# Sparse attention and two MLPs in float32 on one core: the last eight blocks of the first MLP's output as products of quarters

## The chip, the cores and the metric

One core of one Trainium2 chip runs the kernel, in one launch. The metric is the device time of the program in microseconds (us). The kernel before takes 849.72 us, the median of three runs (847.67 to 850.36).

## The reference: what is computed

```python
scores = (1 / sqrt(64)) * q @ k.T            # 4 batches, 8 heads, 576 positions, head size 64
# heads 0-3 see the last 32 positions, heads 4-7 the earlier ones of the same residue mod 32
x = softmax(masked scores) @ v               # -> 2304 tokens x 512
h = x @ moe_w_in                             # first MLP, 512 -> 2048
x = (s * relu(h)**2 + b) @ moe_w_out         # 2048 -> 512, s and b are scalars
h = x @ moe2_w_in                            # second MLP, 512 -> 2048
g = where(h >= 1, h, where(h <= -1, 0, (h + 1)**2 / 4))
out = g @ moe2_w_out                         # 2048 -> 512
```

Everything is float32.

## The kernel before

**Products.** Each float32 operand is split into a high and a low part (hi, lo), and a product is three matmuls on TensorE: hi x hi, hi x lo, lo x hi (`mm3`, L680 to L684; `mm3s`, L929 to L934). The operand that moves is 128 x 384, the weight 128 x 128. ScalarE writes the high part (L310), VectorE or GpSimd subtracts it for the low part (L721, L351, L974).

**Tokens and blocks.** The 2304 tokens are six units of 384 (`UNITS`, NU = 6). The 2048 hidden features are 16 blocks of 128. The first MLP runs in two halves of eight blocks (MS = 8), and each half goes over all units. For one unit and block `hidden` makes the 128 features from the 512 inputs with 12 matmuls (L700), then relu (L704), square (L708 or L710), s and b (L715 or L717), and the split gh, gl (L310, L721). `output` multiplies them into four accumulators of 128 x 384 with 12 matmuls (L751). At the end of the first half the accumulators go to HBM as `part`; in the second half they are read back (`pi`, L745) and added, and the sums are written into x2 (L759), the input of the second MLP.

**Attention** is done in groups, in step with the first units of the first half (`attend_upto`).

**The second MLP** works on pairs of units (three pairs of 2 x 384 tokens) and halves of the features. Each product of 2 x 2 quarters is made as seven products of quarters and of sums of quarters (`PRODS`, Strassen's scheme in Winograd's form): "A11", "A12", "A22", "S1" to "S4" are weights, "B11" to "T4" inputs. `hidden2` and `output2` run them; the running results are combined in one PSUM bank per pair of positions. The sums of the weights are made once: `prepare` (L357 to L396) loads two blocks of raw weights, decodes them (L324 to L332), splits them (L376), forms the sums (L391) and writes all seven quarters, high and low, to HBM (`dw`, L379). Each later use loads one quarter, high and low together, with one 256 KB DMA (L855, rings w0h, w0l, w0hx, w0lx of four, sixteen in all). There are 16 preparations: six in the last unit of the first half (`EARLY`), ten in the second half.

**Raw weights** come as 512 KB loads of integers in two byte planes (`raw`, L324, ring of three), with two decode steps on VectorE (L330, L332) and one on ScalarE (L328).

**What sets the order.** `Issue` collects every operation with its engines, modelled costs, the buffers it needs, and a due time that is worked out backwards from its successors; `order()` takes the operation that can start first (then the one that is due first), and `emit` writes each engine's program in that order. So each engine has a fixed sequence. All of SP's DMAs are issued in order, and an issue that waits for its data or its buffer holds the ones behind it.

The seven products, in the order in which they run:

```python
PRODS = ((1, "A11", "B11"), (5, "S1", "T1"), (6, "S2", "T2"), (3, "S4", "B22"), (7, "S3", "T3"), (2, "A12", "B21"),
         (4, "A22", "T4"))
SUMS = {"T1": ("B11", "B12", "B11"), "T2": ("B11", "B22", "B11"), "T3": ("B12", "B22", "B12"), "T4": ("B21", "B21", "B11")}
```

## Time and profile before

| | |
|---|---|
| median of three runs | 849.72 us (847.67 to 850.36) |
| the profiled execution's own time | 847.82 us |
| its span | 846.0 us, mean granted TensorE clock 0.983 |
| TensorE busy | 824.3 us, 97%, 6336 instructions |
| VectorE busy | 599.4 us, 71%, 1250 instructions |
| ScalarE busy | 517.4 us, 61%, 1054 instructions |
| GpSimd busy | 22.8 us, 3%, 62 instructions |
| DMA | 191.77 MB, mean 227 GB/s |
| second half of the first MLP begins | 287.5 us |
| second MLP begins | 492.2 us |

The profile's busy time counts the durations of instructions; overlapping ones are counted once. PE is TensorE's matmul stream, PEld its weight loads, DVE VectorE, ACT ScalarE, POOL GpSimd, and SP the engine that issues most DMAs. The granted clock is given as a share of 2.4 GHz. The DMA share is the mean busy share of the core's 16 DMA engines.

### The profile page before, as it was taken

To read this page: it belongs to the slowest core of one execution; us is meant where nothing else is said; L and a number is where in the kernel's file an instruction comes from. 1 tells how busy PE (TensorE), PEld (TensorE's weight loads), DVE (VectorE), ACT (ScalarE), POOL (GpSimd) and SP (SyncE) were. 2 spreads that over 40 slices of the span, in tenths; PEclk is the share of its full clock that TensorE was granted. 3 is DMA by queue.
4 is the path that set the end of the run, shared out by engine and by line. 5 is a ranking of instruction groups with operands and counts; after the bars stand their busy time and mean duration, and the time that the engine had idled before them with its cause. 6 is when DMAs were issued, how large, how long until landed. Compare 5 with 4: busy or idle time off the path is not lost.

```text
span 846.0 us, 17391 instructions
## 1 busy us (share of the span) xinstructions
PE 824.3 (97%) x6336; PEld 800.7 (95%) x6336; DVE 599.4 (71%) x1250; ACT 517.4 (61%) x1054; POOL 22.8 (3%) x62
## 2 busy tenths in 40 slices
PE   6789999999999999999999999999999999999998
PEld 3579998989999899999999999999999999999998
DVE  5788647475598785767678356897666998465966
ACT  3577645554577674556567467875477854577653
POOL 1110000010000000000001000000000000000000
PEclk9599999999999999999999999999999999999999
DMA  8858271363389994768785558888988788878883
GB/s 260 259 177 276 99 240 64 91 183 108 122 289 329 277 310 132 223 222 255 257 303 196 154 185 253 252 255 271 293 267 256 252 254 286 289 252 252 251 271 103
DMA packets 115930, 191.77 MB, mean 227 GB/s; under 512 B 13830, under 2 KB 57990, under 8 KB 115846
## 3 DMA queue, kind: packets, MB, share of 16 engines
q1 hardware_dynamic: 114818, 190.23, 70.7%
q8 instruction: 51, 0.84, 0.4%
q10 hardware_dynamic: 1028, 0.43, 0.2%
q14 instruction: 33, 0.27, 0.1%
HBM read 150.25 MB, written 40.37 MB: 225 GB/s over the span
## 4 chain that ended last, share of the span: by engine, by line
PE 84%; DMA 8%; DVE 4%; ACT 2%; issue 1%; SPq 1%; ACTq 0%; DVEq 0%
PE h L682 7%; PE acc L682 6%; PE acc L684 6%; PE acc L683 6%; PE h L683 6%; PE h L684 6%; PE acc L934 6%; PE acc L932 6%; PE acc L933 6%; PE side L934 5%; PE side L933 5%; PE side L932 5%; DMA raw<-in_w_ins 4%; PE h L934 3%; PE h L932 3%; PE h L933 3%
## 5 line engine op out<-in xcount | busy, mean ns | idle before, releaser
L704 ACT ACTIVATE t<-h 128x384 f32<-128x384 f32 x96 | 46.5, 485 | 62.6 <-PE h L684 62.2
L682 PE MATMUL acc<-gh,w1hx 128*128 128x384 f32 x192 | 65.2, 340 | 0.0
L682 PE MATMUL h<-xh,w0hx 128*128 128x384 f32 x192 | 65.1, 339 | 0.0
L683 PE MATMUL acc<-gl,w1hx 128*128 128x384 f32 x192 | 64.9, 338 | 0.2
L683 PE MATMUL h<-xl,w0hx 128*128 128x384 f32 x192 | 64.5, 336 | 0.0
L684 PE MATMUL acc<-gh,w1lx 128*128 128x384 f32 x192 | 64.5, 336 | 0.0
L684 PE MATMUL h<-xh,w0lx 128*128 128x384 f32 x192 | 64.2, 334 | 0.0
L310 ACT ACTIVATE gh<-t 128x384 fp32r<-128x384 f32 x96 | 50.0, 521 | 21.9 <-DVE t L717 21.3
L721 DVE TENSOR_TENSOR gl<-t,gh 128x384 fp32r<-128x384 f32 x92 | 51.0, 555 | 16.1 <-ACT gh L310 15.8
L717 DVE TENSOR_SCALAR t<-t,fix_t 128x384 f32<-128x384 f32 x77 | 36.7, 477 | 35.8 <-ACT t L708 35.5
L682 PE MATMUL acc<-gh,w1h 128*128 128x384 f32 x168 | 57.2, 340 | 0.0
L684 PE MATMUL acc<-gh,w1l 128*128 128x384 f32 x168 | 56.9, 339 | 0.0
L683 PE MATMUL acc<-gl,w1h 128*128 128x384 f32 x168 | 56.8, 338 | 0.0
L682 PE MATMUL h<-xh,w0h 128*128 128x384 f32 x144 | 50.8, 353 | 0.2 <-ACT t L704 0.2
L683 PE MATMUL h<-xl,w0h 128*128 128x384 f32 x144 | 49.4, 343 | 0.0
L684 PE MATMUL h<-xh,w0l 128*128 128x384 f32 x144 | 49.3, 342 | 0.0
L708 ACT ACTIVATE t<-t 128x384 f32<-128x384 f32 x79 | 41.4, 524 | 2.1
L683 PEld LDWEIGHTS acc<-gl,w1hx 128*128 128x128 f32 x192 | 36.0, 188 | 1.1 <-DVE gl L721 1.0
L682 PEld LDWEIGHTS acc<-gh,w1hx 128*128 128x128 f32 x192 | 36.0, 188 | 0.4
L682 PEld LDWEIGHTS h<-xh,w0hx 128*128 128x128 f32 x192 | 36.0, 188 | 0.3
L683 PEld LDWEIGHTS h<-xl,w0hx 128*128 128x128 f32 x192 | 36.1, 188 | 0.0
L684 PEld LDWEIGHTS h<-xh,w0lx 128*128 128x128 f32 x192 | 36.1, 188 | 0.0
(513 smaller groups left out, 2514.3 us busy)
## 6 DMA issues: line engine op xcount, KB each, us to landing
w0h<-dw SPq DMA_DIRECT2D x84, 256.0 KB
w0l<-dw SPq DMA_DIRECT2D x84, 256.0 KB
w0hx<-dw SPq DMA_DIRECT2D x84, 256.0 KB
w0lx<-dw SPq DMA_DIRECT2D x84, 256.0 KB
raw<-in_w_ins SPq DMA_DIRECT2D x32, 512.0 KB
raw<-in_w_outs SPq DMA_DIRECT2D x32, 512.0 KB
dw<-pt SPq DMA_DIRECT2D x48, 256.0 KB
dw<-po SPq DMA_DIRECT2D x48, 256.0 KB
```

What stands on the lines that cost most here:

```text
L310: e.activation(out=out, in_=in_, func=AF.Copy)
L682: e.matmul(out=acc, lhsT=wh, rhs=ah, start=first, stop=False)
L683: e.matmul(out=acc, lhsT=wh, rhs=al, start=False, stop=False)
L684: e.matmul(out=acc, lhsT=wl, rhs=ah, start=False, stop=last)
L704: op(lambda e: e.activation(out=c(t), in_=c(p), func=AF.Relu), [act(n)], [p], [t])
L708: e.activation(out=c(t), in_=c(t), func=AF.Square)
L717: e.tensor_scalar(out=c(t), in0=c(t), scalar1=sb_t[:, 0:1], scalar2=sb_t[:, 1:2], op0=MUL, op1=ADD)
L721: op(lambda e: e.tensor_tensor(out=c(gl), in0=c(t), in1=c(gh).bitcast(F32), op=SUB), [pool(n)] + [dve2(n)], [t, gh], [gl])
L932: e.matmul(out=dst, lhsT=wh, rhs=ah, start=opens and first, stop=False, skip_group_check=not opens)
L933: e.matmul(out=dst, lhsT=wh, rhs=al, start=False, stop=False, skip_group_check=not opens)
L934: e.matmul(out=dst, lhsT=wl, rhs=ah, start=False, stop=last, skip_group_check=not opens)
```

## The change

The last eight blocks of the first MLP are computed in pairs of units. `first_steps(p)` makes the hidden features of a pair directly, as before, but keeps each block's 128 x 384 result whole in SBUF (`inner`: the homes of w_out's weights for pairs 0 and 2; the homes xl of the first units, pi, t and dt for pair 1). `second_steps(p)` then makes the output as the seven products, each over KQ = 4 pairs of blocks with six matmuls (`product`, which `output2` now uses too). Gates are summed for T1 to T4 and every factor is split for each product in which it stands. The partial sums of a unit come into x2 by one DMA (L1021), and the products' running results are added to them (L1034, 14 additions for a pair). Its prepared weights are a third set, dw[2], four preparations more (20 for 16), loaded into a ring of six (`S_TAGS`).

The order of the stages is: first half; hidden of pair 0; outputs of pair 0 between the hidden products of pair 1; outputs of pair 1 between the hidden products of pair 2; outputs of pair 2 alone; second MLP. Seven preparations stand in units 1 to 3 of the first half (`AT_FIRST`), twelve in the last eight blocks (`AT_HALF`), one at the start of the second MLP (`AT_NEXT`). The input weights of the last eight blocks are decoded during the last unit of the first half.

Besides, the planner now knows eight DMAs outstanding (`LANES`), the first batch's side loads of the attention are issued by GpSimd instead of ScalarE and merged into fewer DMAs, fix_t is the first load of ScalarE's queue, po's ring has four buffers instead of two, and the T matrices of the second MLP all stand in the homes xl and xh.

```diff
-EARLY = 6
+KQ = MS // 2
+AT_FIRST = {(1, 6): 1, (2, 0): 1, (2, 3): 1, (2, 6): 1, (3, 1): 1, (3, 4): 1, (3, 7): 1}
+AT_HALF = {(0, 0): 1, (0, 2): 1, (0, 4): 1, (0, 6): 1, (1, 1): 1, (1, 3): 1, (1, 5): 1, (1, 7): 1, (2, 1): 1, (2, 3): 1, (2, 5): 1, (2, 7): 1}
+AT_NEXT = {0: 1}
...
+S_TAGS = ["kb"] * 4 + ["qx", "sx"]
+SPLIT, SUMMED, SUM_BACK, EVAC2 = (0.0, 6.0, 6.0), (0.0, 0.0, 0.0), 0, 5.0
...
+LANES = 8
...
+                    if o.dmas and e != "pool":
+                        at = max(at, lanes[o.dmas - 1] - DMA_ISSUE * (o.dmas - 1))
...
-        op(lambda e: e.dma_start(out=fix_t, in_=fixed[:, 128 + KT:FW]), [("act", 0.5, DMA_LATENCY)], writes=[fix_buf]).sooner = 50.0
-        op(lambda e: [e.dma_start(out=mask_t[g * 64:g * 64 + 54, 0:54], in_=fixed[0:54, 0:54]) for g in range(2)],
-           [("act", 1.0, DMA_LATENCY)], part=[mask_buf[0]]).sooner = 49.0
+        op(lambda e: e.dma_start(out=fix_t, in_=fixed[:, 128 + KT:FW]), [("act", 0.5, DMA_LATENCY)], writes=[fix_buf], dmas=1).sooner = 80.0
+        op(lambda e: e.dma_start(out=mask_t[:, 0:54], in_=bass.AP(fixed.tensor, fixed.offset, [[0, 2], [FW, 64], [1, 54]])),
+           [("act", 0.5, DMA_LATENCY)], part=[mask_buf[0]], dmas=1).sooner = 49.0
...
-        side = ("act", b_line) if b == 0 else ()
+        side = ("pool", b_line) if b == 0 else ()
...
-    def hidden(g, u):
+    def hidden(g, u, whole=None):
         n = UNITS[u]
         p = buf(ps, "h", [128, UMAX], F32, 2)
-        t = buf(sp, "t", [128, UMAX], F32, TB)
-        gh = buf(sp, "gh", [128, UMAX], F32R, LAG + 1)
-        gl = buf(sp, "gl", [128, UMAX], F32R, LAG + 1)
+        if whole:
+            t, own = whole, [whole]
+        else:
+            t = buf(sp, "t", [128, UMAX], F32, TB)
+            gh = buf(sp, "gh", [128, UMAX], F32R, LAG + 1)
+            gl = buf(sp, "gl", [128, UMAX], F32R, LAG + 1)
+            own = [t, gh, gl]
...
+        if o == 2:
+            tag = S_TAGS[loads[1] % len(S_TAGS)]
+            y = buf(sp, tag, [128, 2, 256], F32R, BUFS[tag])
+        else:
+            tag = ("w0h", "w0l", "w0hx", "w0lx")[loads[0] % 4]
+            y = buf(wp, tag, [128, 2, 256], F32R, MS // 2)
+        loads[o == 2] += 1
...
+    blocks = []
+
+    def sum_after(o):
+        return blocks[-SUM_BACK:][:1] if o == 2 and SUM_BACK else ()
+
+    def product(o, k, a, b, g_of, dst):
+        for i in range(counts[o]):
+            home = b
+            if b in SUMS:
+                home, l, r = SUMS[b]
+                d, l, r = (g_of[i, v] for v in (home, l, r))
+                op(lambda e, d=d, l=l, r=r: e.tensor_tensor(out=d.tile, in0=l.tile, in1=r.tile, op=SUB),
+                   [dve2(n), pool(n)], [v for v in (l, r) if v is not d], [d], after=sum_after(o)).sooner = SUMMED[o]
+            g = g_of[i, home]
+            hi = buf(sp, "gh", [128, n], F32R, LAG + 1)
+            lo = buf(sp, "gl", [128, n], F32R, LAG + 1)
+            op(lambda e, g=g, hi=hi: copy(e, hi.tile, g.tile), [act(n)], [g], [hi], allocs=[lo], line=g_line)
+            op(lambda e, g=g, hi=hi, lo=lo: e.tensor_tensor(out=lo.tile, in0=g.tile, in1=hi.tile.bitcast(F32), op=SUB),
+                   [pool(n), dve2(n)], [g, hi], [lo]).sooner = SPLIT[o]
+            w = wmat(o, i, a)
+
+            def f(e, dst=dst, w=w, hi=hi, lo=lo, k=k, i=i):
+                for c in range(2):
+                    wc = [w.tile[:, v, c * 128:(c + 1) * 128] for v in range(2)]
+                    mm3s(e, dst[c].tile, wc, (hi.tile, lo.tile), k in START, i == 0, i == counts[o] - 1)
+
+            pe_block(f, [w, hi, lo], dst)
+            blocks.append(chain[0])
+            yield
+
+    halves, spares, mixed = [{} for _ in range(PAIRS)], {}, []
+
+    def spare(tag):
+        if tag not in spares:
+            spares[tag] = const.tile([128, KD, NP], F32, name=f"g_{tag}", tag=tag)
+        return spares[tag]
+
+    def inner(p, m, u):
+        if p != 1:
+            return buf(wp, ("w1h", "w1l")[u % 2] + ("" if m < KQ else "x"), [128, n], F32, MS // 2)
+        j = 2 * m + u % 2
+        if j < 2 * KD:
+            return Part(lambda: spare(f"xl{j // KD}")[:, j % KD, :])
+        tag = (["pi"] * KD + ["t"] * TB + ["dt"])[j - 2 * KD]
+        return buf(sp, tag, [128, n], F32, {"pi": KD, "t": TB, "dt": DT}[tag])
+
+    def first_steps(p):
+        us = (2 * p, 2 * p + 1)
+        for g in range(MS, 2 * MS):
+            m = g - MS
+            make(0, g + 1)
+            for u in us:
+                y = halves[p][m % KQ, f"B{m // KQ + 1}{u % 2 + 1}"] = inner(p, m, u)
+                hidden(g, u, y)
+                if pend:
+                    output(*pend.pop(0))
+                yield
+            for _ in range(AT_HALF.get((p, m), 0)):
+                prepare(*todo.pop(0))
+
+    def second_steps(p):
+        us = (2 * p, 2 * p + 1)
+        slot = {u: [Buf(None, None) for _ in range(KD)] for u in us}
+        for u in us:
+            op(lambda e, u=u: e.dma_start(out=x2[u].tile, in_=part_d[u].rearrange("c p n -> p c n")), [dma(KD * n * 512)],
+               part_buf[u], slot[u], after=[x_last[u]], allocs=[x2[u]])
+        sets = [[buf(ps, t, [128, NP], F32, 2 if t == "side" else 1) for t in ts]
+                for ts in (("side", "side"), ("acc0", "acc1"), ("acc2", "acc3"))]
+        x, z, y = sets[p % 3:] + sets[:p % 3]
+        for k, a, b in PRODS:
+            dst = {1: x, 6: x, 7: x, 4: x, 5: z, 3: z, 2: y}[k]
+            yield from product(2, k, a, b, halves[p], dst)
+            r, t, ends = {1: (1, 0, 0), 5: (2, 1, 0), 6: (1, 1, 0), 3: (1, 1, 1), 7: (2, 1, 1), 2: (1, 0, 1), 4: (2, 0, 1)}[k]
+            u = us[t]
+            for c in range(2):
+                j = c + 2 * (r - 1)
+                d = slot[u][j]
+                op(lambda e, u=u, j=j, s=dst[c]: e.tensor_tensor(out=x2[u].tile[:, j, :], in0=s.tile, in1=x2[u].tile[:, j, :],
+                                                                 op=ADD),
+                   [dve(n)], [dst[c]], [d], part=touched(u, j) if ends else ()).sooner = EVAC2
...
+            if u == NU - 1:
+                make(0, MS + g + 1)
+            for _ in range(AT_FIRST.get((u, g), 0)):
+                prepare(*todo.pop(0), early=u < NU - 1)
...
+    list(first_steps(0))
+    for p in range(PAIRS):
+        more, done_, step = first_steps(p + 1) if p + 1 < PAIRS else iter(()), 0, 0
+        for _ in second_steps(p):
+            step += 1
+            while done_ < step * 2 * MS / (7 * KQ):
+                next(more, None)
+                done_ += 1
+        list(more)
+        if p == 1:
+            mixed.append(chain[0])
```

SP's queue in the last eight blocks. Before, writes of prepared weights (dw), raw loads and the partial sums of one unit:

```order
L745 DMA pi_5380<-part_79 128x384
L745 DMA pi_5393<-part_79 128x384
L745 DMA pi_5399<-part_79 128x384
L745 DMA pi_5410<-part_79 128x384
L324 DMA raw_5420<-in_w_outs 128x512
L379 DMA dw_2_92<-pt_5412 128x2x256
L379 DMA dw_2_92<-po_5413 128x2x256
L379 DMA dw_3_93<-po_5429 128x256
L379 DMA dw_3_93<-pt_5428 128x256
L379 DMA dw_2_92<-pt_5479 128x2x256
L379 DMA dw_3_93<-pt_5486 128x2x256
L379 DMA dw_2_92<-po_5480 128x2x256
```

After, the same queue while pair 1's outputs are made: the loads of kb, qx and sx are the prepared weights of the products (dw_0 to dw_3 of the third set), between the writes of others:

```order
L851 DMA kb_5968<-dw_2_100 128x512
L851 DMA kb_5978<-dw_3_101 128x512
L394 DMA dw_3_93<-po_5906 128x2x256
L394 DMA dw_3_93<-po_5893 128x2x256
L394 DMA dw_4_94<-pt_5992 128x256
L394 DMA dw_4_94<-po_5993 128x256
L851 DMA qx_6025<-dw_0_98 128x512
L394 DMA dw_4_94<-pt_6010 128x2x256
L851 DMA sx_6043<-dw_1_99 128x512
L394 DMA dw_4_94<-po_6011 128x2x256
L851 DMA kb_6073<-dw_2_100 128x512
L851 DMA kb_6089<-dw_3_101 128x512
```

Loads that TensorE waits for soon now stand behind writes that wait for ScalarE's pt and VectorE's po.

VectorE in the last eight blocks. Before, affines (L717), splits gl (L721) and the steps of the preparations (L330, L332, L376):

```order
L717 TENSOR_SCALAR t_5490<-t_5490,fix_t 128x384
L376 TENSOR_TENSOR po_5544<-sm_5341,pt_5543 128x512
L721 TENSOR_TENSOR gl_5492<-t_5490,gh_5491 128x384
L330 TENSOR_SCALAR qv_5518<-qv_5518 128x512
L710 TENSOR_TENSOR t_5537<-t_5537 128x384
L332 SCALAR_TENSOR_TENSOR qv_5518<-raw_5517,qv_5518 128x512
L376 TENSOR_TENSOR po_5571<-sm_5340,pt_5570 128x512
L721 TENSOR_TENSOR gl_5539<-t_5537,gh_5538 128x384
L330 TENSOR_SCALAR qv_5519<-qv_5519 128x512
L376 TENSOR_TENSOR po_5606<-qv_5518,pt_5605 128x256
L332 SCALAR_TENSOR_TENSOR qv_5519<-raw_5560,qv_5519 128x512
L717 TENSOR_SCALAR t_5586<-t_5586,fix_t 128x384
```

After, at the same place of the program (L735 affine, L974 split of a product's factor, L351 and L353 decode, L391 and L406 preparation, L1034 addition of a result to x2):

```order
L406 TENSOR_TENSOR qv_5497<-qv_5497,qv_5496 128x256
L351 TENSOR_SCALAR sm_5695<-sm_5695 128x512
L353 SCALAR_TENSOR_TENSOR sm_5695<-raw_5694,sm_5695 128x512
L735 TENSOR_SCALAR w1l_5715<-w1l_5715,fix_t 128x384
L974 TENSOR_TENSOR gl_5759<-pi_5111,gh_5758 128x384
L351 TENSOR_SCALAR sm_5696<-sm_5696 128x512
L974 TENSOR_TENSOR gl_5774<-pi_5212,gh_5773 128x384
L353 SCALAR_TENSOR_TENSOR sm_5696<-raw_5697,sm_5696 128x512
L391 TENSOR_TENSOR po_5781<-qv_5497,pt_5780 128x512
L391 TENSOR_TENSOR po_5789<-qv_5496,pt_5788 128x512
L1034 TENSOR_TENSOR x_3_5449<-acc_948_5454,x_3_5449 128x384
L1034 TENSOR_TENSOR x_3_5449<-acc_949_5455,x_3_5449 128x384
```

The splits are now one for each product block, and the additions stand between them.

SP's queue at the start, with the semaphores that an issue waits for in brackets. Before:

```order
L447 DMA xh_2_131<-in_strd 128x764 x2
L447 DMA w0hx_148<-in_strd 54x2x256 x2
L447 DMA xl_15_157<-in_strd 128x2x764 [waits DMAHW0_49]
L447 DMA w0lx_193<-in_strd 54x2x256 [waits DMAHW5_49]
L447 DMA w0lx_193<-in_strd 54x2x256 [waits DMAHW7_49]
L447 DMA xh_37_203<-in_loc 128x896 [waits DMAHW1_49]
L447 DMA xl_38_236<-in_loc 128x896 [waits DMAHW4_49]
```

After:

```order
L461 DMA xh_2_134<-in_strd 128x764 x2
L461 DMA w0hx_153<-in_strd 54x2x256 x2
L461 DMA xl_15_166<-in_strd 128x2x764
L461 DMA w0lx_196<-in_strd 54x2x256
L461 DMA w0lx_196<-in_strd 54x2x256 [waits DMAHW0_49]
L461 DMA xh_37_203<-in_loc 128x896 [waits DMAHW1_49]
L461 DMA xl_38_236<-in_loc 128x896 [waits DMAHW2_49]
```

The load of xl and the first half of the load of w0lx lose their waits; the other waits are for other lanes.

## Rows read from the trace of the kernel before

**Rows 1.** Page: busy time by engine; the chain that ended last, by engine.
```profile
PE 824.3 (97%) x6336; PEld 800.7 (95%) x6336; DVE 599.4 (71%) x1250; ACT 517.4 (61%) x1054; POOL 22.8 (3%) x62
...
PE 84%; DMA 8%; DVE 4%; ACT 2%; issue 1%; SPq 1%; ACTq 0%; DVEq 0%
```

**Rows 2.** Busy by stretch: us, PE, PEld, DVE, ACT, POOL, PEclk, DMA share, GB/s.
```profile
42.00:120.00 78.00, 74.58 (x797) 70.07 (x796) 56.61 (x126) 52.08 (x117) 6.60 (x15) 0.95 0.60 194
...
293.00:493.00 200.00, 197.78 (x1131) 196.52 (x1130) 141.71 (x280) 121.50 (x235) 5.42 (x5) 1.00 0.69 223
```

**Rows 3.** Timeline of PE, output matmuls: start us, duration us, instruction.
```profile
469.77 0.34 PE L682 MATMUL acc<-gh,w1h 128*128 128x384 f32 x1
...
471.16 0.34 PE L684 MATMUL acc<-gh,w1l 128*128 128x384 f32 x1
```

**Rows 4.** Busy by stretch of 30 us around 300 us.
```profile
270.00:300.00 30.00, 27.79 (x156) 26.79 (x156) 25.09 (x52) 22.00 (x45) 0.00 (x0) 1.00 0.94 296
300.00:330.00 30.00, 29.78 (x168) 28.84 (x167) 21.83 (x45) 18.86 (x38) 0.00 (x0) 1.00 0.63 211
330.00:360.00 30.00, 30.00 (x174) 30.00 (x174) 20.22 (x42) 16.16 (x31) 0.00 (x0) 1.00 0.68 217
```

**Rows 5.** Chain of waits, 230 to 335 us: start us, us, what.
```profile
275.07 8.14 DMA raw<-in_w_ins
...
297.74 4.90 DMA raw<-in_w_ins
```

**Rows 6.** Busy by stretch, where the transfers are heaviest.
```profile
255.00:265.00 10.00, 10.00 (x60) 10.00 (x59) 7.48 (x17) 6.44 (x15) 0.00 (x0) 1.00 1.01 353
275.00:285.00 10.00, 10.00 (x59) 9.77 (x58) 6.83 (x14) 6.30 (x14) 0.00 (x0) 1.00 1.00 301
260.00:280.00 20.00, 20.00 (x117) 20.00 (x116) 15.93 (x33) 13.85 (x28) 0.00 (x0) 1.00 0.98 320
250.00:290.00 40.00, 40.00 (x231) 39.65 (x230) 33.24 (x71) 27.70 (x56) 0.00 (x0) 1.00 0.95 312
```

**Rows 7.** DVE groups by form: shapes, count, busy us, mean ns, idle before.
```profile
L721 DVE TENSOR_TENSOR gl<-t,gh 128x384 fp32r<-128x384 f32 x92 | 51.0, 555 | 16.1 <-ACT gh L310 15.8
L717 DVE TENSOR_SCALAR t<-t,fix_t 128x384 f32<-128x384 f32 x77 | 36.7, 477 | 35.8 <-ACT t L708 35.5
L332 DVE SCALAR_TENSOR_TENSOR dt<-raw,dt 128x512 int32<-128x512 int32 x32 | 22.0, 688 | 0.3
L818 DVE TENSOR_TENSOR tm<-x,tm 128x768 fp32r<-128x768 f32 x18 | 17.0, 954 | 0.6 <-ACT tm L310 0.6
L376 DVE TENSOR_TENSOR po<-sm,pt 128x512 fp32r<-128x512 f32 x24 | 16.4, 689 | 3.4 <-ACT pt L310 2.2 <-ACT gh L310 0.7 <-DMA dw<-po 0.4
L759 DVE TENSOR_TENSOR x<-acc,pi 128x384 f32<-128x384 f32 x24 | 12.2, 553 | 3.6 <-PE acc L684 3.6
L330 DVE TENSOR_SCALAR dt<-dt 128x512 int32<-128x512 int32 x32 | 13.4, 420 | 4.6 <-ACT dt L328 4.5
L391 DVE TENSOR_TENSOR sm<-sm,sm 128x256 f32<-128x256 f32 x19 | 8.0, 421 | 0.2
```

**Rows 8.** Timeline of DVE: four additions of L759 in a row.
```profile
395.41 1.94 DVE L759 TENSOR_TENSOR x<-acc,pi 128x384 f32<-128x384 f32 x4
```

**Rows 9.** Busy by stretch, in the second MLP.
```profile
540.00:570.00 30.00, 30.00 (x175) 30.00 (x174) 29.49 (x56) 22.75 (x46) 0.00 (x0) 1.00 0.81 254
```

**Rows 10.** Timelines of SP's queue and of PE, the first 8 us.
```profile
3.91 0.40 SPq L447 DMA_DIRECT2D xl<-in_strd  x1
7.00 0.72 SPq L447 DMA_DIRECT2D w0lx<-in_strd  x2
...
7.44 0.39 PE L562 MATMUL acc<-bias_t,idb_t 128*128 128x256 bf16 x2 [2.18 <-DVE idb_t L312]
```

**Rows 11.** Timeline of DVE: a multiply while GpSimd works.
```profile
51.79 1.51 DVE L600 TENSOR_TENSOR sm<-sm,dn 128x512 f32<-128x512 f32 x1
```

**Rows 12.** Waits of SP's queue: line, waited for, total us, times, longest.
```profile
SPq L379 <- ACT pt L310: 57.1, 35, 6.2
```

More of the change, by code (lines that the diff above doesn't have):

```diff
@@ L88 @@
 class Op:
-    __slots__ = ("fn", "engs", "deps", "succ", "allocs", "bufs", "due", "wait", "ready", "start", "eng", "n", "behind", "sooner", "idle")
+    __slots__ = ("fn", "engs", "deps", "succ", "allocs", "bufs", "due", "wait", "ready", "start", "eng", "n", "behind", "sooner", "idle", "dmas")
 class Issue:
@@ L202, in order @@
             end = at + d + lag
+            if o.dmas and e != "pool":
+                lanes = sorted(lanes[o.dmas:] + [end] * o.dmas)
             for b in o.allocs:
@@ L1021, in sparse_attention_two_mlps @@
     for u, g0, g1 in segments:
-        earlier, last = seen[u] > 0, g1 == 2 * MS
+        earlier = seen[u] > 0
         seen[u] += 1
```

207 lines of the change are left out of this document (78 added, 129 removed).

## Prediction, made before the changed kernel ran

> **What bounds the kernel now.** I read the page's busy shares first, then the chain that ended last, then tables by stretch, then single instructions where a term needs a price. TensorE (PE) is busy 824.3 of 846.0 us, VectorE (DVE) 71% and ScalarE 61% [rows 1]; the chain that ended last is PE for 84% and DMA for 8% [rows 1]. So PE's instruction count is the bound, and what it waits for is small. In the stage that the change rewrites, the second half of the first MLP, PE works 197.78 of 200 us, DVE 141.71, the transfers have a share of 0.69 at 223 GB/s [rows 2]. How fast PE goes there is read from its starts, not from its durations: eight steps of the 128x384 matmul lie between 469.77 and 471.16, 0.1735 us each, while a row says 0.34 [rows 3]. A window of 30 us that is full holds 174; the stretch from 270 to 300 holds 156 and that from 300 to 330 holds 168 [rows 4]. There the chain runs over loads of raw weights, 8.14 us for one at 275.07 and 4.90 at 297.74 [rows 5], at a DMA share of 0.94 [rows 4]. So the kernel has one known hole, made by transfers, of (18 + 6) x 0.1735 = 4.2 us.
>
> **The change, part by part.** The execution that I sum against took 847.82 us (span 846.0 and 1.8 around it); the median of the runs is 849.72, 1.9 above it, and I add those 1.9 at the end.
>
> *Matmuls removed.* In the last eight blocks every unit and block had 12 output matmuls, 6 x 8 x 12 = 576. Now a pair of units has 7 products x 4 blocks x 6 = 168, three pairs 504. 72 go, none is added, all of one shape: 72 x 0.1735 = -12.5 us [rows 3]. Nothing lies over them, because PE is the chain. If PE turns out to wait in this stage, this is the term that is eaten.
>
> *The hole at 270 to 330.* Six weight preparations stood in the last unit of the first half, with their raw loads and writes; seven are now spread over units 1 to 3, and unit 5 only decodes the eight next input weights. I take the whole hole as gone, -4.2; bounds 0 and -4.2, since each raw load is still there, only elsewhere.
>
> *The start.* SP's first loads are issued at 3.91 and 7.00 us, with idle time between; the first scores start at 7.44 after 2.18 us of waiting for idb_t [rows 10]. The first batch's side loads leave ScalarE's queue for GpSimd's, the waits of SP's third and fourth load go in the order of instructions, and fix_t (which makes idb_t) is issued first. I take -1.5; bounds 0 (the loads still need their time to land) and -3 (the idle time between SP's issues).
>
> *VectorE's work.* Added are 36 splits gl of 0.555 (84 for 48), 48 sums of the gates, 18 more additions of results (42 for 24) of 0.553, and four more preparations. One preparation is two decodes whose longer step is 0.688, three splits of 0.689 and one half as wide, and about four sums of 0.421 [rows 7]: near 6.3 us with their short steps. From the fourth product block to the last split DVE has by the order 161 instructions of 128x384 (81 splits, 40 sums, 40 additions), 24 affines, 32 decode steps, 30 splits of weights, 27 sums of weights and 7 of 128x768; by their durations [rows 7] about 158 us. PE's work over the same blocks is 146 us. That would be a new bound, if durations added up. Four additions in a row, 0.553 each, took 1.94 us: (4 x 0.553 - 1.94) / 3 = 0.09 us of each lies under the next [rows 8]. 281 instructions x 0.09 = 25, so 133 us against 146. The same is seen in the second MLP, where DVE is busy 29.49 of 30 us by durations and PE still issues 175 matmuls [rows 9]. In the last pair alone, with no hidden products beside it, it is 57 instructions of 128x384 and 6 of 128x768: 57 x 0.463 + 6 x 0.86 = 31.6 us against 28 x 6 x 0.1735 = 29.1, less the lead of three blocks (3.1) that the ring of gl gives. I take +2; bounds 0 and +10 (158 less 146, less some lead).
>
> The Trainium skill speaks against my reading: "VectorE: DVE Perf Modes", section "The DRAIN you can't avoid", says that the next instruction does not start until the pipe of the one ahead is empty. By that the durations add, and the stage would end about 8 us later than in my sum. "Perfetto Trace Analysis", section "Optimizing Scalar/DVE Operations", says that the write acknowledgement of a profiled instruction overlaps the next; rows 8 agree with the second, for instructions that follow each other without a wait.
>
> *Transfers.* New are 84 loads of 256 KB (one for every product block), 84 writes of 256 KB by the 12 preparations that stand in this half, and one 768 KB load per unit for the partial sums. Between the seventh of those 84 loads and the last, SP issues 78 loads (20.4 MB), 71 writes (16.3 MB), 18 raw loads (9.4 MB) and 4 loads of partial sums (3.1 MB), 49 MB. A load can be issued when the block six before it is done, so this lies in 82 product blocks and the hidden blocks of two pairs: (82 x 6 + 384) x 0.1735 = 152 us, 324 GB/s. The trace shows 353 GB/s for one stretch of 10 us and 301 for another, both at a full share, 320 over 20 us and 312 over 40 us [rows 6]. At 353 it is hidden; at 320 it takes 154 us, +2; at 312, 158, +6; at 301, 164, +12. The longest stretch is nearest to what is asked for, so +6. Then the queue itself: SP issues in order, and writes wait for ScalarE's copies, 57.1 us in 35 waits, the longest 6.2 [rows 12]. The product loads stand behind such writes now, and six blocks give a lead of 6.2 us; a few misses cost +2. Together +8, bounds 0 and +20 (301 GB/s, and twelve preparations with 0.7 us lost at each).
>
> The Trainium skill has a faster figure: "DMA: Bandwidth & Descriptors", section "Measured", gives 425 GB/s for a core that streams alone in 16 MB transfers. By it no transfer here would be late. The rows of this case, mostly of 256 and 512 KB, do not come near it: 320 GB/s goes with a share of 0.98 [rows 6].
>
> *Attention's stretch.* Seven preparations, 7 x 6.3 = 44 us of DVE work, move to units 1 to 3, where DVE had 56.61 of 78 us [rows 2]; GpSimd has 26 rows more, and a 128x512 multiply on DVE took 1.51 us while GpSimd ran [rows 11]. I take +1.5; bounds 0 and +4 (five such stretched instructions).
>
> *Sum.* 847.8 - 12.5 - 4.2 - 1.5 + 2 + 8 + 1.5 = 841.1, and with 1.9 for the median 843.
>
> **The rivals.**
> A: everything new is hidden. For it: DVE's 133 us lie under 146, and the chip shows 353 GB/s for 10 us. Against it: 324 GB/s wanted for 152 us and no row of 40 us above 312. 847.8 - 12.5 - 4.2 - 1.5 + 1.5 + 1.9 = 833.
> B: DVE is the bound of the stage, as durations would have it. For it: 158 us against 146. Against it: rows 8 and 9. The forecast with +10 for DVE in the place of +2: 851. This is the skill's first rule above, told as rows.
> C: the gain is eaten by plain lack of bandwidth, 301 GB/s throughout: +12 for +6, and the hole at 270 does not close (+4.2): 853 less what no longer waits at the start of the second MLP, so 848 to 853. For it: the full share at 301 [rows 6]. Against it: it is the lowest of four.
> D, slower: SP's order. A write that waits for ScalarE or DVE holds the product loads behind it beyond the lead of 6.2 us. Without any transfer term the sum is 835 with the median's 1.9; slower begins at 852.3, so it decides from 17 us, 1.4 us lost at each of 12 preparations. At 2 us each it gives 835 + 24 = 859. For it: a mean wait of 57.1 / 35 = 1.6 us now, with one of 6.2 [rows 12], and a third more to copy. Against it: today's waits cost PE nothing after 300 us, and the writes become ready earlier than the loads they stand ahead of.
> That the matmuls do not go is no rival: the order has 72 fewer.
>
> **How the numbers follow.** Forecast 843 (its own range 837 to 847): 0.42. A: 0.22. B: 0.07. C: 0.15. D: 0.14. What a measurement of this kernel can tell is about 0.3%, 2.5 us, so faster is below 847.2 and slower above 852.3. Faster: all of A and nearly all of the forecast and a little of B and C, 0.66. Slower: D and a few of B and C, 0.17. Same: 0.17. The range goes from 832, the low end of A with the start's -3 in part, to 855: it leaves out most of D's far half and what lies below 832, together under 2 in 10.
>
> **What would show it.** In the trace after: full windows of 30 us still hold 174 matmuls between 270 and 330 (the hole gone). First scores before 7 us (the start). In the second half, PE's matmuls per 30 us: 174 throughout is A; 165 to 170 with the waits of the product lines put down to DMA kb, qx and sx is the forecast or C; put down to gl on DVE, with DVE without idle time, is B; loads issued late by SP, with SP waiting for ScalarE's pt ahead of them and a DMA share well under 0.9, is D. I am wrong in kind if PE's pitch changes, if PE waits for the additions to free its banks, or if the new waits lie in the second MLP.

## The result: 855.25 us, slower

The changed kernel takes 855.25 us (median of seven runs, 851.42 to 858.16) against 850.26 for the kernel before on the same chip: a ratio of 1.0064, 95% interval 1.0037 to 1.0090, so 0.6% slower. The forecast was 843, faster. The profiled execution took 856.34 us and has a span of 854.6 us.

The page after: the busy times [rows 1], and the clock in 40 slices.

```profile
PE 814.8 (95%) x6260; PEld 787.9 (92%) x6263; DVE 643.4 (75%) x1351; ACT 533.5 (62%) x1102; POOL 57.5 (7%) x89
...
PEclk7797999999999999999999999999999999999999
```

TensorE is busy 9.5 us less than before, and the span is 8.6 us longer. So about 18 us of waiting are new. Where they lie is read by stretches (columns as in [rows 2]); the lines answer to [rows 2], [rows 4] and [rows 6]:

```profile
42.00:120.00 78.00, 70.39 (x823) 65.18 (x823) 55.21 (x125) 48.80 (x108) 10.31 (x18) 0.91 0.57 181
120.00:232.00 112.00, 104.81 (x1323) 96.30 (x1322) 78.46 (x197) 64.01 (x138) 17.04 (x31) 1.00 0.72 227
270.00:300.00 30.00, 30.00 (x174) 30.00 (x174) 20.69 (x40) 20.00 (x38) 0.00 (x0) 1.00 0.56 194
300.00:330.00 30.00, 30.00 (x174) 29.77 (x173) 19.90 (x43) 18.92 (x39) 0.00 (x0) 1.00 0.54 174
360.00:390.00 30.00, 30.00 (x173) 30.00 (x172) 26.25 (x56) 21.34 (x44) 1.01 (x1) 1.00 1.01 351
450.00:480.00 30.00, 27.84 (x148) 26.71 (x147) 25.70 (x52) 17.91 (x36) 5.26 (x4) 0.94 0.91 310
480.00:510.00 30.00, 28.99 (x163) 27.73 (x162) 29.48 (x54) 16.88 (x33) 6.90 (x3) 1.00 1.00 341
```

Three things are to be seen. The hole at 270 to 330 is gone, 174 matmuls in each window. The heaviest transfers, 351 GB/s over 30 us, run beside a full TensorE (173). But TensorE is short in the attention's stretch (70.39 of 78 and 104.81 of 112 us, where it had 74.58 and 111.96), and 450 to 480 holds 148 matmuls, 480 to 510 holds 163.

The start, as in [rows 10]: timeline of PE and of VectorE.

```profile
15.04 0.59 PE L576 MATMUL acc<-bias_t,idb_t 128*128 128x256 bf16 x2 [9.69 <-DVE bias_t L333]
```

```profile
14.79 0.20 DVE L333 CAST bias_t<-mask_t 128x64 bf16<-128x64 f32 x1 [9.71 <-DMA mask_t<-in_fixed]
```

The first scores begin at 15.04 us, not before 7. They wait for bias_t, and that for the mask's load. Of what the forecast built on, SP's third and fourth loads did go out earlier (2.44 and 2.96 us, before 3.91 and 7.00); the first scores do not hang on them.

To add the losses up I number the matmuls of the two MLPs in the order in which TensorE runs them (the expectations below say "triple" for this number by mistake, each is a single matmul; only their 26th, 71st and 73rd triple or group are of three matmuls, so matmul 78, 213 and 219). The table gives, from each trace, the start of matmul 0 and the time for each stretch of numbers (the last one to the start of the last matmul; 96 to 144 takes 8.3 us in all). Matmuls 0 to 1152 are the first half, with the attention between them up to about 780; 2304 before is the start of the second MLP, after it is 2232. The outputs of the last pair alone are 2064 to 2232 in the changed order; at 0.1735 us a matmul they would take 29.1 us, and 1728 to 2064 would take 58.3. "raw" is what ScalarE stood waiting for raw loads from 144 to 864.

| run | start of 0 | 0-48 | 48-96 | 144-864 | raw | 864-1152 | 1152-1728 | 1728-2304 | of it to 2064 | last pair | 2304-end |
|---|---|---|---|---|---|---|---|---|---|---|---|
| before | 41.5 | 16.0 | 15.6 | 156.0 | 1.7 | 50.3 | 104.2 | 100.3 | - | - | 350.0 |
| after | 43.5 | 14.8 | 22.5 | 163.7 | 19.3 | 50.0 | 101.5 | 107.2 | 59.3 | 35.5 | 339.0 |
| e1_old_start | 43.1 | 13.2 | 15.4 | 161.2 | 12.0 | 50.0 | 100.7 | 110.3 | 63.3 | 33.7 | 340.3 |
| e2_old_mask | 43.2 | 14.9 | 22.8 | 163.0 | 16.4 | 50.0 | 101.0 | 106.2 | 59.0 | 34.7 | 338.5 |
| e3_early_dma | 43.7 | 14.9 | 22.5 | 162.3 | 17.0 | 50.0 | 100.8 | 108.3 | 62.5 | 33.2 | 339.5 |
| e4_one_early | 43.6 | 15.1 | 23.3 | 161.7 | 6.0 | 50.0 | 101.5 | 107.6 | 60.3 | 34.8 | 339.9 |
| e5_act_merged | 43.5 | 14.8 | 23.0 | 162.5 | 17.9 | 50.0 | 101.3 | 106.9 | 59.0 | 35.4 | 339.1 |
| e6_unmerged | 44.4 | 15.1 | 15.3 | 163.5 | 12.0 | 50.0 | 101.7 | 113.2 | 62.4 | 38.3 | 340.6 |
| e7_raw_late | 40.2 | 21.6 | 12.0 | 156.9 | 0.0 | 54.0 | 100.7 | 109.1 | 59.0 | 37.6 | 351.7 |
| e8_raw_late_new_start | 46.0 | 19.6 | 10.3 | 157.1 | 0.0 | 50.7 | 100.7 | 104.9 | 59.0 | 32.0 | 356.0 |
| e9_twenty_early | 43.7 | 18.1 | 9.9 | 156.6 | 0.0 | 64.4 | 100.7 | 110.9 | 59.0 | 39.4 | 338.3 |
| e10_raw_kept | 42.6 | 14.3 | 14.4 | 158.7 | 9.0 | 50.0 | 100.7 | 104.8 | 59.0 | 33.0 | 337.9 |
| e11_late_dma | 40.6 | 13.9 | 16.9 | 160.0 | 12.8 | 50.0 | 100.7 | 106.2 | 59.0 | 33.9 | 337.4 |
| e12_old_start_one_early | 43.7 | 14.2 | 14.3 | 156.0 | 0.0 | 50.0 | 101.2 | 108.4 | 59.7 | 36.1 | 338.0 |
| e13_late_raw_told | 40.2 | 13.5 | 15.4 | 159.5 | 11.5 | 50.0 | 100.7 | 105.7 | 59.0 | 33.6 | 341.6 |
| e14_no_port | 44.6 | 13.3 | 15.4 | 158.5 | 7.6 | 50.0 | 100.7 | 105.8 | 59.0 | 33.7 | 342.2 |
| e15_early_later | 43.8 | 13.2 | 15.4 | 159.4 | 6.2 | 50.0 | 100.7 | 106.0 | 59.0 | 33.8 | 340.1 |
| e16_before_merged | 40.9 | 14.8 | 22.6 | 155.1 | 1.0 | 50.0 | 103.5 | 100.3 | - | - | 350.0 |
| e17_none_in_second | 43.5 | 13.7 | 15.3 | 159.8 | 10.5 | 50.0 | 100.7 | 107.3 | 59.0 | 34.0 | 337.4 |

After against before: +2.0 at the start, -1.2, +7.0 in 48 to 96, +7.7 in 144 to 864, -0.3, -2.7 (the hole), +6.9 in 1728 to 2304, and -11.0 to the end (12.5 removed, 1.5 given back): +8.4 in all.

Each row is one execution, and some lie well off their median: e6's is the slowest of twelve (857.96 us, median 851.51), e13's the fastest of twelve (840.55, median 843.28). e1, e10, e11 and e13 have the same first half and differ there by up to 2.9 us at matmul 0 and 2.5 in 144 to 864, so a difference of that size between two rows shows nothing by itself.

### The profile page after: what moved, and what is told of

It reads as the page before. It is cut to its first block, busy times and chain, and to the rows that moved or that the text cites. A ratio compares the mean times of both kernels' runs of the same rounds, so it can differ in the third digit from the quotient of the medians.

```text
span 854.6 us, 17660 instructions
## 1 busy us (share of the span) xinstructions
PE 814.8 (95%) x6260; PEld 787.9 (92%) x6263; DVE 643.4 (75%) x1351; ACT 533.5 (62%) x1102; POOL 57.5 (7%) x89
## 5 line engine op out<-in xcount | busy, mean ns | idle before, releaser
L698 PE MATMUL h<-xh,w0lx 128*128 128x384 f32 x192 | 64.4, 336 | 0.0
L349 ACT ACTIVATE dt<-raw 128x512 f32<-128x512 f32 x38 | 25.4, 668 | 28.0 <-DMA raw<-in_w_outs 14.8
L331 ACT ACTIVATE gh<-w1h 128x384 fp32r<-128x384 f32 x54 | 27.7, 522 | 19.0 <-PE acc L931 11.3
L696 PEld LDWEIGHTS h<-xh,w0h 128*128 128x128 f32 x192 | 36.7, 191 | 3.1 <-ACT xh L331 2.5
L697 PEld LDWEIGHTS h<-xl,w0h 128*128 128x128 f32 x192 | 36.7, 191 | 0.9 <-DVE xl L679 0.9
L698 PEld LDWEIGHTS h<-xh,w0l 128*128 128x128 f32 x192 | 36.6, 191 | 0.0
L735 DVE TENSOR_SCALAR t<-t,fix_t 128x384 f32<-128x384 f32 x34 | 17.1, 503 | 24.1 <-ACT t L726 24.1
L696 PE MATMUL acc<-gh,w1h 128*128 128x384 f32 x96 | 33.7, 351 | 0.0
L696 PE MATMUL acc<-gh,w1hx 128*128 128x384 f32 x96 | 33.2, 346 | 0.0
L331 ACT ACTIVATE gh<-w1hx 128x384 fp32r<-128x384 f32 x46 | 24.1, 523 | 14.5 <-PE acc L931 7.8
L697 PE MATMUL acc<-gl,w1h 128*128 128x384 f32 x96 | 32.6, 340 | 0.0
L698 PE MATMUL acc<-gh,w1l 128*128 128x384 f32 x96 | 32.6, 339 | 0.0
```

The costliest lines, as they stand in the source:

```text
L331: e.activation(out=out, in_=in_, func=AF.Copy)
L349: first = op(lambda e: e.activation(out=x(), in_=words(1).bitcast(F32), func=AF.Prelu, scale=2.0 ** -112, alpha=-2.0 ** 32), [act(DM)], [r ...
L696: e.matmul(out=acc, lhsT=wh, rhs=ah, start=first, stop=False)
L697: e.matmul(out=acc, lhsT=wh, rhs=al, start=False, stop=False)
L698: e.matmul(out=acc, lhsT=wl, rhs=ah, start=False, stop=last)
L735: e.tensor_scalar(out=c(t), in0=c(t), scalar1=sb_t[:, 0:1], scalar2=sb_t[:, 1:2], op0=MUL, op1=ADD)
```

## The experiments

Medians from different chips are not compared; what is compared is the ratio to the kernel before on the same chip, with its 95% interval, and the stretches of the table (one execution each).

**e1_old_start, e2_old_mask, e3_early_dma, e4_one_early.** The edits:

```diff
# e1: side = ("act", b_line); the merged attention loads split as before; mask loads first, then fix_t
# e2: only the mask: two loads issued first, then fix_t
# e3: in prepare(early=True) no decode, split, sum: raw loads, and writes of a zeroed po
# e4: only the first early prepare is made; dw[o][i] of the six others points to its result
```

> The changed kernel with the start of the one before: the first batch's side loads on ScalarE's queue again and unmerged, the two mask loads first, then fix_t. The seven preparations stay in units 1 to 3. Theory S (the start costs about 6.5 us: first scores at 15.04 instead of 7.44, and the first 144 matmul triples of the first MLP end 7.8 us later than before): first scores near 7.5, the 144th triple near 81 to 83, and 855.3 - 6.5 = 849 us. Theory P (the preparations amid the attention cost about 9 us, the start is made good later): 853 to 855. Rival O (the planner's new rule of eight transfers has changed the whole order, no single part matters): 853 or more.

> The changed kernel with one edit: the mask comes by two loads issued first, as before, and not by one merged load behind fix_t. GpSimd's queue still has the side loads. If the merged mask load alone makes the late start: first scores near 7.5 and 849 us, as in the run with the whole old start. If it is GpSimd's queue that delays everything: mask still lands after 10 us, 854 to 856.

> The changed kernel, the seven early preparations reduced to their transfers: 14 raw loads and the writes of the same bytes stay, but nothing is decoded, split or summed (the written weights are zeros, so the products with them are left out of the result). Theory P by VectorE and ScalarE: between the 288th and the 864th matmul triple 125 us instead of 134, and 855.3 - 8 = 847. Theory P by the transfers (raw loads in front of the attention's loads): 132 to 134 us there, 854 or more. Theory S and rival O: 853 or more.

> The changed kernel with one early preparation instead of seven; the other six sets of weights are not made, their loads read the first one's. Theory P: about six sevenths of the 9 us come back, 847. Theory S: 854 to 856. Rival O: no more than 2 us, 853 or more. It should be no slower than the run that keeps the transfers; the difference between them is what the transfers cost.

Measured: e1 846.86 us, 0.9975 (0.9952 to 0.9997); e2 855.78, 1.0082 (1.0064 to 1.0100); e3 858.05, 1.0134 (1.0098 to 1.0170); e4 855.79, 1.0082 (1.0059 to 1.0105). Theory S holds for the start as a whole and falls for the mask: e2 has its first scores at 8.95 us, and its time is that of the changed kernel. The late first scores themselves are made up until matmul 0 (43.2 there, 43.5 after, and 43.1 in e1, whose first scores come at 7.30). Theory P falls as a matter of work: without it (e3) and with six preparations fewer (e4) the total gains nothing. e3 is even slower than the changed kernel, why stays open; from matmul 288 to 864 it takes 132.6 us, which is what was expected if raw loads in front of the attention cost the time. What e1 takes away is in 48 to 96, 15.4 us for 22.5. The planned order of e1 differs there: the tenth attention group (of 21) stands behind matmul 213 of the first MLP, as in the kernel before, in the changed kernel and e2 to e4 behind matmul 78.

**e5_act_merged, e6_unmerged**, one part of the start each, and **e7_raw_late, e8_raw_late_new_start**:

```diff
# e5: -side = ("pool", b_line)   +side = ("act", b_line), costs as for ScalarE's queue
# e6: the merged attention loads (k3, vb_) split as before, nothing else
# e7 (on e1) and e8 (on after), in decode():
-[dma(src.shape[0] * src.shape[1] * 8)]
+[late(src.shape[0] * src.shape[1] * 8)]      # lag DMA_LATENCY + 4.0
```

> The changed kernel, only the first batch's side loads go back from GpSimd's queue to ScalarE's; they stay merged, and the tenth attention group still stands behind the 26th output or hidden group of the first MLP (behind the 71st in the kernel before and in the run with the whole old start). Theory G (the early place of the tenth group costs the 7 us between the 48th and the 96th triple): 22 us there as in the changed kernel, 854 us. Theory Q (GpSimd's queue costs them, its loads land 8 us after issue): first scores earlier, 15 us there, 848 us.

> The changed kernel, only the merged attention loads are split again as before; the side loads stay on GpSimd's queue and the mask stays one load behind fix_t. In this order the tenth attention group stands behind the 71st group. Theory G: the 48th to the 96th triple take 15 to 16 us instead of 22, and 855.3 - 6 = 849 us although the first scores come late, at about 15 us. Theory Q: 22 us there and 854 to 856.

> The kernel with the old start (846.9 us); in addition the planner is told that a raw load lands 4 us later (its guess was 2 us of latency, the traced one took 7.01 us); no work is changed, only the order. Theory W (in the second half ScalarE stands at the decode of a raw load that is late, VectorE stands behind ScalarE, the splits gl behind that, and TensorE waits and falls to half its clock): the stretches from the 1728th to the 2304th triple lose less, 102 instead of 110 us, and 846.9 - 6 = 841 us. Rival V (VectorE has simply too much to do there): no more than 2 us, 845 to 848.

> The changed kernel as it is, with the new start, and the planner told of 4 us more for a raw load. Its order has the tenth attention group behind the 73rd group. Theory G with W: both losses shrink, 855.3 - 6 - 5 = 844 us. Theory Q with W: 850. Theory V with Q: 855.

Measured: e5 854.34, 1.0073 (1.0045 to 1.0100); e6 851.51, 1.0034 (1.0013 to 1.0055); e7 856.48, 1.0104 (1.0083 to 1.0126); e8 858.47, 1.0125 (1.0097 to 1.0153). GpSimd's queue is cleared of the loss in 48 to 96 (e5: 23.0 us), not of the late first scores: in e5 they come at 8.12 us, with the mask's load as in the changed kernel, so either edit alone (e2, e5) brings them forward. Unmerging alone puts the tenth group back, and 48 to 96 takes 15.3 us although the first scores come at 13.79; the total gives back only a part, and its interval overlaps the changed kernel's. e7 and e8 missed in the total. e7 missed in its stretch too (109.1 us in 1728 to 2304, not 102), e8 hit there (104.9) and in 48 to 96. In both 144 to 864 takes 157 us with all seven early preparations, but TensorE waits elsewhere, in the second MLP. Waits of PE (line, waited for, total us, times, longest) of e7 and of e8:

```profile
PE side L931 <- ACT gh L331: 8.2, 1, 8.2
```

```profile
PE side L930 <- DMA w0h<-dw: 7.1, 2, 5.6
PE h L930 <- DMA w0lx<-dw: 2.9, 1, 2.9
```

**e9 to e12.** The edits:

```diff
# e9 (on e8):  -AT_NEXT = {0: 1}  +AT_NEXT = {}   and (4, 2): 1 added to AT_FIRST
# e10 (on e1): later preparations after the first decode its two raw tiles again, no raw load
# e11 (on e1): e3's edit for the thirteen later preparations
# e12 (on e1): e4's edit
```

> The new start and 4 us more for raw loads, as in the run of that name (858.5 us), and the twentieth preparation is moved from the start of the second MLP to unit 4 of the first half. Theory N (there TensorE waited 7.1 and 2.9 us for product weights that this preparation writes just before they are loaded, and lost 14 us with the half clock behind them): the second MLP's first 432 triples lose nothing, 858.5 - 12 = 846 us. If those waits had another cause: 855 or more.

> The kernel with the old start (846.9 us), but only the first of the thirteen later preparations loads its raw weights; the others decode the same two tiles again, so their weights are wrong in value while all decoding, splits, sums and writes stay. This takes the late raw loads away and leaves VectorE's and ScalarE's work. Theory W (late raw loads stop ScalarE, then VectorE, then TensorE): from the 1728th to the 2304th triple 101 to 103 us instead of 110, 846.9 - 8 = 839 us. Rival V (too much work on VectorE): 108 to 110 us there, 845 to 847.

> The kernel with the old start, the thirteen later preparations reduced to transfers: raw loads and writes of zeros stay, nothing is decoded, split or summed (so most products are left out of the result's value). Rival V: from the 1728th to the 2304th triple 100 to 102 us, 838 us. Theory W in its strict form (each raw load still has a reader on ScalarE that the gates' copies stand behind): 105 to 110 us and 843 or more.

> The kernel with the old start and one early preparation instead of seven; the other sets read the first one's weights. With the new start this changed nothing (855.8 for 855.3). Theory P2 (seven early preparations cost 5 us between the 144th and the 864th triple, 161.2 for 156.0 before, which shows once the start is out of the way): 156 to 157 us there and 842 to 843. If the 5 us are the order's and not the work's: 160 or more and 846.

Measured: e9 858.77, 1.0120 (1.0095 to 1.0145); e10 838.19, 0.9877 (0.9848 to 0.9906); e11 839.30, 0.9883 (0.9858 to 0.9909); e12 841.36, 0.9908 (0.9880 to 0.9936). In the totals e10 came out near theory W's figure, e11 near rival V's and e12 near theory P2's; in the stretch from 1728 to 2304 e10 missed (104.8, not 101 to 103), and e11's 106.2 is in W's range, not V's. e9 is a miss: the second MLP loses nothing now (338.3), but the eighth early preparation holds up the raw loads of the next input weights, and TensorE stands once for 12.4 us in front of the second half:

```profile
PE h L697 <- ACT w0h L331: 12.4, 1, 12.4
```

Theory W, in the run it is about (e1), as the chain of waits shows it, with the same instructions in the timelines of ScalarE and VectorE:

```profile
423.63 7.01 DMA raw<-in_w_outs
430.67 0.67 ACT qv L349
431.36 0.44 DVE qv L351
...
433.32 0.48 DVE gl L975
433.84 0.45 PE acc L931
```

```profile
430.67 0.66 ACT L349 ACTIVATE qv<-raw 128x512 f32<-128x512 f32 x1 [3.41 <-DMA raw<-in_w_outs]
```

```profile
431.36 0.43 DVE L351 TENSOR_SCALAR qv<-qv 128x512 int32<-128x512 int32 x1 [3.85 <-ACT qv L349]
```

```profile
430.00:435.00 5.00, 3.40 (x18) 2.81 (x17) 3.61 (x8) 3.26 (x7) 0.00 (x0) 0.99 1.03 377
435.00:440.00 5.00, 5.00 (x21) 5.00 (x21) 5.00 (x12) 3.46 (x7) 0.98 (x1) 0.67 0.61 202
```

A raw load issued at 423.63 needs 7.01 us; ScalarE, whose next instruction is its decode, stands 3.41 us, VectorE behind it 3.85, TensorE waits for the split gl, and after the wait its granted clock is half for a while (0.67 over 435 to 440 us; ten starts there are 0.32 us apart, not 0.1735). With the raw loads gone (e10), or the work gone (e11), 420 to 450 is full. The next windows are not, in either (e1 first, then e10, then e11):

```profile
420.00:450.00 30.00, 28.39 (x151) 27.70 (x150) 22.94 (x50) 16.80 (x35) 0.98 (x1) 0.94 0.93 303
450.00:480.00 30.00, 27.98 (x154) 26.11 (x153) 29.80 (x57) 19.98 (x40) 5.26 (x4) 1.00 0.97 331
```

```profile
420.00:450.00 30.00, 30.00 (x173) 30.00 (x172) 27.95 (x58) 21.19 (x42) 1.56 (x2) 1.00 0.79 244
450.00:480.00 30.00, 27.58 (x153) 25.91 (x151) 28.75 (x54) 16.97 (x32) 3.28 (x2) 1.00 0.88 272
```

```profile
420.00:450.00 30.00, 30.00 (x173) 30.00 (x172) 16.04 (x32) 15.86 (x35) 1.93 (x3) 1.00 0.90 293
450.00:480.00 30.00, 27.68 (x150) 25.48 (x149) 28.06 (x56) 14.00 (x29) 0.70 (x2) 1.00 1.02 351
```

So both theories hold, each in its place: late raw loads around 430 in e1, and at 450 to 480, where the last pair has no hidden products beside it, VectorE at 28 to 30 of 30 us even with no preparation's work at all (e11). That second loss is some 20 to 25 matmuls, 4 us.

In the changed kernel itself the first of the two losses is not there: up to matmul 2064 it takes 59.3 us, e1 63.3, and 59.0 where the raw loads are gone or told (e10, e13). It loses in the last pair, 35.5 us for 29.1. There VectorE is busy for 34.56 of 35.50 us; the rows are the changed kernel, e10 and e11, each over its own last pair:

```profile
463.50:499.00 35.50, 32.34 (x170) 30.33 (x169) 34.56 (x64) 18.96 (x36) 10.94 (x6) 0.95 0.95 321
```

```profile
448.00:481.00 33.00, 30.58 (x170) 28.91 (x169) 31.75 (x59) 18.97 (x36) 3.28 (x2) 1.00 0.89 275
```

```profile
449.40:483.30 33.90, 31.35 (x169) 28.83 (x169) 31.92 (x62) 16.06 (x33) 1.30 (x2) 1.00 1.02 351
```

About 4 of these 6.4 us stay in e10 and e11, and 2.9 or more in every run. That it is VectorE's work is argued from its busy time and not shown by a run: [rows 9] have 29.49 of 30 us with TensorE full, no run takes the splits and sums of the products away, and TensorE's short waits there are for the splits gl, the copies gh and product weights by turns.

e12 shows 156.0 us in 144 to 864, the time of before.

The raw loads also settle where most of the 7.7 us of that stretch come from. The column "raw" goes with its time: 19.3 us of ScalarE's waits in the changed kernel and 163.7 us, none in e7, e8, e9 and e12 and 156 to 157 us, with one, seven or eight preparations. e8 is the changed kernel with nothing but the planner's landing time changed: 157.1. The longest wait stands in front of the first early preparation. The rows are ScalarE and TensorE in the changed kernel, then the same two in e4:

```profile
138.27 0.66 ACT L349 ACTIVATE dt<-raw 128x512 f32<-128x512 f32 x1 [6.73 <-DMA raw<-in_w_outs]
```

```profile
142.59 0.60 PE L576 MATMUL side<-bias_t,idb_t 128*128 128x256 bf16 x2 [2.33 <-DVE sx L607]
```

```profile
138.77 0.66 ACT L349 ACTIVATE dt<-raw 128x512 f32<-128x512 f32 x1 [6.05 <-DMA raw<-in_w_outs]
```

```profile
142.76 0.70 PE L576 MATMUL side<-bias_t,idb_t 128*128 128x256 bf16 x2 [2.87 <-DVE sx L607]
```

ScalarE stands 6.73 us at the decode, VectorE 6.84 us behind it, so the scores are read late and TensorE cannot write the next ones. e4 keeps this one early preparation, and with it the wait.

**e13, e14, e15.** Here the work is whole again:

```diff
# e13 (on e1): decode(..., lag): 4.0 us more for the raw loads of preparations 8 to 19 only
# e14 (on e13): [dve2(256), pool(256)] -> [dve2(256)] for the sums of weights
# e15 (on e13): AT_FIRST = {(2, 0), (2, 4), (3, 0), (3, 4), (4, 0), (4, 3), (4, 6)}
```

> The kernel with the old start (846.9 us), the planner told of 4 us more for the raw loads of the twelve preparations in the last eight blocks alone (the earlier try told it of all raw loads, and the last preparation came too late in the second MLP). All work and all transfers stay; up to the last eight blocks the order is the same. Theory W: matmul 1728 to 2304 in 103 to 106 us instead of 110, 846.9 - 5 = 842 us. Rival V (VectorE's work there): 109 or more, 846 to 848.

> As the run before it in this list (raw loads told later), and the sums of weights in the preparations go to VectorE alone, never to GpSimd. In the changed kernel VectorE's instructions took 0.9 to 1.1 us instead of 0.55 while GpSimd made such sums (463 to 469 us). Theory X (that shared time is part of the loss): 2 to 3 us better than with GpSimd. If not: within 1.5 us.

> As the first of this list, and three of the seven early preparations go from units 1 to 3 to unit 4, where the attention is done. Theory P2 (preparations amid the attention cost up to 5 us): matmul 144 to 864 in 158 us instead of 161, 2 to 3 us better than the first of this list; rival: their transfers delay the raw loads of the next input weights in unit 5, as in the run with an eighth early preparation, and matmul 864 to 1152 takes more than 52 us.

Measured: e13 843.28, 0.9949 (0.9925 to 0.9973); e14 843.88, 0.9942 (0.9920 to 0.9964); e15 841.69, 0.9928 (0.9905 to 0.9951). With the same work, transfers and first half as e1, e13 takes 105.7 us for 110.3 in 1728 to 2304, all of it in front of the last pair (59.0 for 63.3), which is W's share of e1; in the total the intervals of e13 and e1 overlap, so by time alone it is likely and not certain. e14 against e13 is no difference: beside GpSimd's sums single VectorE instructions are longer (one split and one sum of the changed kernel, 0.98 and 1.09 us where 0.55 is usual), but that is not what the time hangs on.

```profile
466.12 0.98 DVE L974 TENSOR_TENSOR gl<-w1h,gh 128x384 fp32r<-128x384 f32 x1
...
467.84 1.09 DVE L968 TENSOR_TENSOR w1h<-w1l,w1h 128x384 f32<-128x384 f32 x1
```

e15 against e13 is within the intervals too; its stretch 144 to 864 is 159.4 for 159.5, so its expectation is not confirmed; its rival falls too (50.0 us in 864 to 1152).

**e16_before_merged, e17_none_in_second.**

```diff
# e16 (on before): only the k3 and vb_ loads of the attention merged, as in the changed kernel
# e17 (on e15): AT_NEXT = {}, and (0, 1): 1 added to AT_HALF
```

> The kernel before, its only edit the merged attention loads of the changed one (ScalarE's queue, the mask and everything of the MLPs stay). Its order now has the tenth attention group behind the 26th triple of matmuls of the first MLP instead of the 71st. Theory G: matmul 48 to 96 take 22 us instead of 15.4, and the kernel takes 848.5 + 5 = 853 to 854 us. If the early place costs something only together with the new work: 848 to 850.

> The kernel of e15_early_later (841.7 us) with the last preparation moved from the start of the second MLP into the last eight blocks (thirteen there). There matmul 2592 to 2736 take 27 us instead of 25, with TensorE waiting behind gl. If that is this preparation's work: 2 us less there; but thirteen preparations in 187 us make 2304 arrive later, so 840 to 843 in all.

Measured: e16 852.64, 1.0059 (1.0042 to 1.0076); e17 838.60, 0.9892 (0.9871 to 0.9912). e16 shows theory G outside the change: merging a few small loads costs the kernel before 5 us (ratio times 848); 48 to 96 takes 7.0 us longer, and no other stretch does. The timeline of PE in e16, and then in the changed kernel, has the same two waits:

```profile
67.94 0.43 PE L623 MATMUL side<-pt,qv 36*64 36x36 f32 x4 [2.81 <-issue]
```

```profile
70.54 0.43 PE L637 MATMUL side<-pt,qv 36*64 36x36 f32 x4 [2.82 <-issue]
...
74.70 0.69 PE L696 MATMUL h<-xh,w0h 128*128 128x384 f32 x1 [2.38 <-ACT xh L331]
```

The windows are of e16:

```profile
68.00:72.00 4.00, 1.27 (x24) 0.98 (x24) 1.80 (x4) 1.76 (x5) 0.00 (x0) 0.50 1.01 379
72.00:76.00 4.00, 3.17 (x9) 2.77 (x10) 3.88 (x12) 2.68 (x9) 0.94 (x1) 0.50 0.72 213
```

What holds the two up is seen on VectorE and ScalarE, here in the changed kernel:

```profile
70.04 0.40 DVE L607 TENSOR_TENSOR sm<-side,mx 128x256 f32<-128x256 f32 x1
```

```profile
72.58 0.66 ACT L349 ACTIVATE dt<-raw 128x512 f32<-128x512 f32 x1 [3.15 <-DMA raw<-in_w_ins]
...
74.17 0.69 ACT L331 ACTIVATE xh<-side 128x36 fp32r<-128x36 f32 x4
```

The scores of the tenth group now stand in front of the values of the ninth. Both use the ring `side`, which has two buffers, so the values wait until VectorE is done with the scores: its last read of the first buffer ends at 70.44, and the values begin at 70.54. Then ScalarE stands 3.15 us at the decode of a late raw load, and the copy xh that TensorE waits for is behind it (e16 has the same wait, 3.37 us). TensorE stands 2.8 and 2.4 us, and runs at 0.50 of its clock. e17 came out below its range (840 to 843), and 2592 to 2736 takes 25.0 us for 26.9 in e15. It is the version that beats both kernels: 1.1% faster than before, with all the work done.

## Why the prediction was wrong, point by point

Two steps failed: the start, whose merged loads were priced at nothing beyond the first loads, and the attention's stretch, priced by VectorE's work. Against the profiled execution (856.3 us, the sum said 841.1) the table gives 9.3 of the 15.2 us to what comes before matmul 96 and 6.2 to matmuls 144 to 864; what is left nearly cancels.

- *Matmuls removed, -12.5*: right. The end of the table has 11.0 less, and 337.4 (12.6 less) in e17.
- *The hole, -4.2*: right in kind, -3.0 to -3.8 (1152 to 1728 takes 101.5 and 100.7 for 104.2, 864 to 1152 another 0.3 less).
- *The start, -1.5*: wrong in sign and in reason. First scores come 7.6 us later, the mask's load being what they wait for. Matmul 0 comes 2.0 us later, but not because of them: it does so in e1 and e2 as well. The step that failed is to read the new start as a matter of the first ten microseconds: through the planner the merging moved the tenth attention group from behind matmul 213 to behind matmul 78, worth +7.0 us in 48 to 96 (e6, e16), or 5.7 from 0 to 96. That could have been read from the order, and I read the order at the start and in the last eight blocks only.
- *Attention's stretch, +1.5, bounds 0 to 4*: +7.7, and wrong in reason. The term was VectorE's 44 us of work and a few stretched instructions; what cost the time is that ScalarE stood 19.3 us at raw loads that the planner expected earlier, with VectorE and the scores behind it. With the landing time told, seven preparations cost 1.1 us there (e8 against before). e12 against e1 gives 5.2 us to six of the seven with the old landing time.
- *VectorE, +2, bounds 0 to 10*: right in place, too small: the last pair loses 6.4 us in the changed kernel, and 4 to 5 in e10, e11, e13 to e15 and e17. The lead of 3.1 us that was to cover the pair is not there when it begins: ScalarE has just stood 3.56 us at a raw load (456.09), and the pair takes 35.5 us, not 31.6; without that wait it still takes 33.0 (e10). The durations' bound, 10, is not reached. The Trainium skill's rule in "VectorE: DVE Perf Modes", section "The DRAIN you can't avoid", does not show here: five splits, sums and additions of 0.55 us in a row, 462.85 to 465.19 us, start 0.47 us apart. The same section says that a next instruction that is not held starts earlier, which the prediction left out; read whole, it does not speak against the prediction's overlap.
- *Transfers, +8*: wrong step. Lack of bandwidth was priced at +6; the chip gave 351 GB/s over 30 us with TensorE full, and e10, without the later raw loads, has the last pair only 0.9 us shorter than e11 with all of them, so of that term little is to be seen. The Trainium skill's 425 GB/s ("DMA: Bandwidth & Descriptors", section "Measured") is not reached by any window shown here, but its direction was the better one. The queue's price, +2 for product loads behind writes, did not come either (no long wait of TensorE for kb, qx or sx in the last eight blocks of the changed kernel). Raw loads do cost, by another door: ScalarE and VectorE stand behind them. In the last eight blocks that is some 2.5 us of the changed kernel (the last pair's 35.5 us against 33.0 in e10); most of it is in the attention's stretch.
- *The rivals*: the time is between C and D. C's cause did not happen. That the forecast is only 12 us off is partly luck: the 8 us set aside for transfers were hardly needed for them and made up for losses that the sum did not have. D's mechanism, an in-order queue in front of a wait, did, on ScalarE's and VectorE's queues and not on SP's. The price that no rival had was the order of the first 100 matmuls.
